# One load instead of two for the query weights, three instead of two for the bias row, in a one-core decode kernel

## Chip, core and metric

The kernel runs on one core of a Trainium2 chip. The time is device microseconds for one execution; lower is better. The core's engines are TensorE (PE), VectorE (DVE), ScalarE (ACT), GpSimd (POOL) and SyncE (SP, which here only issues loads). Data comes from HBM through 16 DMA engines that the core's queues share.

## What is computed

Two branches on the same eight token rows, mixed by a gate. All tensors are bf16.

```python
g = sigmoid((x * gate_w).sum(-1, keepdims=True))        # x: 8 x 1 x 448
q = (x @ wq)                                            # wq: 448 x 4096, 16 heads of 256
k, v = last 1024 of 4096 positions, 8 kv heads, each for 2 query heads
a = softmax(q @ k^T / 16) @ v, then @ wo                # wo: 4096 x 448
b = gelu(layernorm(x) @ w1 + b1) @ w2 + b2              # 448 -> 1792 -> 448
out = g * a + (1 - g) * b
```

## The kernel before, in words

**What is loaded.** Each of the eight batch rows needs 4 MB of keys and 4 MB of values, 64 MB in all. The weights add wq (3.5 MB), wo (3.5 MB), w1 and w2 (1.5 MB each). Nearly everything is read once from HBM.

**The ring of slots.** All large loads go through `ring`, four slots of 32 KB per partition. A list `plan` holds loaders in order: wq, k0, k1, v0, k2, v1, ... k7, v6, w1, v7 with w2, wo. `pump` (L98) issues loaders as long as no more than four slots are unconsumed; `done` (L104) is called by the code that has read a slot, and pumps the next loader. All these loads are issued by SP, in this order, so an issue that waits for a free slot holds every later one of SP's. `half_loader` (L115), `pair_loader` (L125) and `rows_loader` (L137) are the three shapes; the DMA issues stand on L121, L131 and L142. A key or value load is 256 rows of 16 KB.

**Completion semaphores.** In the trace's records the loads of SP and ACT take eight completion semaphores in turn: x, wq's first part, gate_w, wq's second part, wq's last part, k0's two halves, k1, and then the first again for v0, and so on. A load whose semaphore is still in use by an earlier one can't be issued until that one has landed. In the middle of the kernel this never binds; at the end, six of wo's eight pieces wait for it.

**wq.** Its first 384 rows are put three to a partition, `wq_m`, 128 rows of 24 KB that lie one behind the other in HBM. L155 cuts this in two column ranges: the first third (8 KB a row, 1 MB) and the other two thirds (16 KB a row, 2 MB). The last 64 rows of wq (`wq_t`, 128 rows of 4 KB) are a third load. `rows_loader` issues one DMA for each piece.

**The query.** `moments` (L253) turns x into the matmul's stationary tile `xw`. `query` (L383) then runs 24 matmuls of 128x512 on L389, eight for each third of `wq_m`, then four on L401 for `wq_t`, calls `done`, and spreads the result into `qw` (L411 to L427, on ACT and DVE). `gate` (L261) reads g_b, the gate weights that ACT loaded with L185.

**A batch row.** `transpose_keys` (L351) turns the keys, in part by POOL copies (L346), in the main by PE transposes (L370) that ACT (L376) and DVE (L378) copy out of PSUM. `scores` (L429), `top`, `expo`, `turn`, `scale` and `bring` give the softmax, `values` (L501) the product with v. The steps of row b-1 are put between the key blocks of row b, by `steps` (L598).

**The bias row.** `biases` (L189) runs once among row 1's key blocks: SP issues b2 (L190) and then b1 on L194. b1's 1792 elements go as four pieces of 448 elements (896 bytes) to partitions 0, 32, 64 and 96 of `b1_r`, in two loads of two pieces each. `norm` (L303) reads both in row 2 (L317, L318).

**The end.** After the last values, the wide products with w2 and wo accumulate in PSUM, the last chunks in two column halves (L679); L689 adds them, and SP and ACT store a half each (L691).

Of the kernel before, what the change touches and what calls it, by code (L numbers as in the profile page):

```python
# [17 lines left out]
def kernel(  # L18
# [20 lines left out]
    HD = A_wq.shape[1]  # L39
# [6 lines left out]
    QD = 4  # L46
    BL = P // QD
    NJ = Dh // P
    NR = 3
# [97 lines left out]
    wq_m = A_wq[0:DM, :].rearrange("(p r) n -> p (r n)", r=NR)  # L147
# [4 lines left out]
    wo_v = A_wo.rearrange("(q p j) n -> p q (j n)", p=P, j=J8)  # L152
    OW1T = NR * F
    OW2 = OW1T + FH
    wq_r = [wq_m[:, 0:HD], wq_m[:, HD : NR * HD]]  # L155

    def last_values(t):
        pair_loader(A_v_cache, NB - 1, 2)(t)
# [25 lines left out]
    b1_r = consts.tile([P, FQ], BF16)  # L184
# [4 lines left out]
    def biases():  # L189
        nc.sync.dma_start(  # L190
            b2_b[:], B_b2.rearrange("(o d) -> o d", o=1).to_broadcast([NB, D])
        )
        for t in range(0, QD, 2):
            nc.sync.dma_start(  # L194
                b1_r[BL * t : BL * (t + 2) : BL, :],
                B_b1.rearrange("(t d) -> t d", t=QD)[t : t + 2, :],
            )

    ident = consts.tile([P, P], BF16)
# [522 lines left out]
```

## Time and profile before

| what | value |
|---|---|
| time, median of 3 runs | 189.98 us (189.89 to 190.21) |
| time of the profiled execution | 189.76 us |
| its span, first to last instruction | 188.0 us |
| PE busy / DVE / ACT / POOL | 65% / 51% / 49% / 35% of the span |
| loads and stores | 77.85 MB, mean 414 GB/s over the span |
| share of the SP and ACT load queues: SP's queue (q1), ACT's (q10) | 97.3%, 0.0% of 16 engines' span |
| mean granted TensorE clock | 0.873 |

The profiled execution took 1.76 us more than its span; that part lies outside the first and last instruction. Busy times of different engines overlap, so they don't add up to the span. The share of a DMA queue is the time of its packets over the time of all 16 DMA engines.

### The profile page before, as it was taken

To read this page: it belongs to the slowest core of one execution; us is meant where nothing else is said; L and a number is where in the kernel's file an instruction comes from. 1 tells how busy PE (TensorE), PEld (TensorE's weight loads), DVE (VectorE), ACT (ScalarE), POOL (GpSimd) and SP (SyncE) were. 2 spreads that over 40 slices of the span, in tenths; PEclk is the share of its full clock that TensorE was granted. 3 is DMA by queue.
4 is the path that set the end of the run, shared out by engine and by line. 5 is a ranking of instruction groups with operands and counts; after the bars stand their busy time and mean duration, and the time that the engine had idled before them with its cause. 6 is when DMAs were issued, how large, how long until landed. Compare 5 with 4: busy or idle time off the path is not lost.

```text
span 188.0 us, 2799 instructions
## 1 busy us (share of the span) xinstructions
PE 122.3 (65%) x1104; PEld 79.8 (42%) x1104; DVE 96.5 (51%) x166; ACT 91.4 (49%) x115; POOL 66.4 (35%) x143
## 2 busy tenths in 40 slices
PE   0273099598598447991695948923968885353972
PEld 0022096395296216750684336503853662110221
DVE  7306514754287926740673248713763773763511
ACT  2006879598249255862287059620891994010000
POOL 8000093291069505800398039100991840000000
PEclk9999759969969997999579699995799999955599
DMA  6999999999999999999999999999999999999991
GB/s 211 448 411 439 446 422 422 436 443 422 422 439 424 420 436 439 422 422 439 436 425 425 443 432 418 429 443 436 411 436 446 415 425 428 416 429 441 412 402 54
DMA packets 6771, 77.85 MB, mean 414 GB/s; under 512 B 588, under 2 KB 1128, under 8 KB 1896
## 3 DMA queue, kind: packets, MB, share of 16 engines
q1 hardware_dynamic: 6712, 77.68, 97.3%
q8 instruction: 8, 0.13, 0.2%
q10 hardware_dynamic: 48, 0.02, 0.0%
q14 instruction: 3, 0.02, 0.0%
HBM read 77.69 MB, written 0.01 MB: 413 GB/s over the span
## 4 chain that ended last, share of the span: by engine, by line
DMA 76%; PE 13%; POOL 5%; DVE 2%; ACT 1%; issue 1%; SPq 0%; POOLq 0%; DVEq 0%
DMA slot<-in_A_k_cache_dram 51%; DMA slot<-in_A_v_cache_dram 12%; DMA slot<-in_A_wo_dram 9%; PE ktp L370 8%; POOL kt L346 5%; DMA slot<-in_A_wq_dram 5%; DVE kt L378 1%; PE S_ps L435 1%; ACT kt L376 1%; PE S_ps L389 1%; PE S_ps L401 1%; PE PO L506 1%; DVE B L338 1%; PE S_ps L679 0%; SPq L142 0%
## 5 line engine op out<-in xcount | busy, mean ns | idle before, releaser
L370 PE MATMUL ktp<-ident_f,slot 128*128 128x128 f32 x468 | 73.3, 314 | 33.3 <-DMA slot<-in_A_k_cache_dram 21.2
L346 POOL COPY kt<-B 32x128 f32<-32x128 f32 (+1 forms) x128 | 62.1, 485 | 85.9 <-DVE B L338 80.9
L376 ACT COPY kt<-ktp 128x1024 bf16<-128x1024 bf16 x77 | 73.3, 1030 | 27.4 <-PE ktp L370 27.0
L370 PEld LDWEIGHTS ktp<-ident_f,slot 128*128 128x128 f32 x468 | 61.4, 162 | 47.9 <-issue 21.6
L378 DVE COPY kt<-ktp 128x1024 bf16<-128x1024 bf16 x40 | 27.5, 687 | 19.0 <-PE ktp L370 18.9
L435 PE MATMUL S_ps<-kt,qw 128*4 128x512 bf16 x256 | 17.4, 412 | 7.6 <-POOL kt L346 6.2
L506 PE MATMUL PO<-slot,ET 128*16 128x512 bf16 x256 | 17.5, 416 | 7.3 <-DMA slot<-in_A_v_cache_dram 7.3
L453 ACT ACTIVATE E<-S_ps,nmx 128x1024 f32<-128x1024 f32 x8 | 8.9, 1114 | 22.9 <-DVE nmx L448 22.9
L448 DVE TENSOR_REDUCE nmx<-S_ps 128x1 f32<-128x1024 f32 x8 | 9.8, 1224 | 17.9 <-PE S_ps L435 17.9
L338 DVE STREAM_TRANSPOSE B<-slot 128x512 f32<-128x512 f32 (+1 forms) x8 | 7.3, 908 | 21.2 <-DMA slot<-in_A_k_cache_dram 21.2
L506 PEld LDWEIGHTS <-ET 128*16 128x16 bf16 x256 | 7.1, 94 | 16.8 <-issue 11.0
L435 PEld LDWEIGHTS <-qw 128*4 128x4 bf16 x256 | 5.9, 85 | 16.0 <-issue 10.6
L462 DVE STREAM_TRANSPOSE EB<-E 128x1056 f32<-128x1056 f32 x8 | 10.2, 1278 | 0.3
L389 PE MATMUL S_ps<-slot,xw 128*8 128x512 bf16 x24 | 2.9, 617 | 9.4 <-DVE xw L239 6.0
L522 DVE STREAM_TRANSPOSE T<-PO 128x512 f32<-128x512 f32 x8 | 5.6, 703 | 3.6 <-PE PO L506 3.6
L489 DVE TENSOR_TENSOR ET<-sm,mask 128x512 bf16<-128x512 f32 x8 | 5.5, 692 | 3.4 <-PE sm L481 3.4
L414 DVE STREAM_TRANSPOSE qt<-qs 128x512 bf16<-128x512 bf16 x2 | 1.3, 690 | 8.7 <-ACT qs L411 8.7
L389 PEld LDWEIGHTS <-xw 128*8 128x8 bf16 x24 | 0.6, 100 | 10.7 <-POOL b_r L222 5.9
L584 ACT ACTIVATE zb<-za 128x448 f32<-128x448 f32 x1 | 0.6, 577 | 8.5 <-DVE za L583 8.5
L651 PE MATMUL warm<-slot,ident 128*128 128x512 bf16 (+1 forms) x12 | 4.6, 475 | 0.0
L411 ACT ACTIVATE qs<-S_ps 128x1024 bf16<-128x1024 f32 x1 | 1.0, 1023 | 7.3 <-PE S_ps L401 7.3
L468 DVE SCALAR_TENSOR_TENSOR EZ<-EB,gall 128x128 bf16<-128x128 f32 x8 | 4.0, 495 | 0.0
(81 smaller groups left out, 57.6 us busy)
## 6 DMA issues: line engine op xcount, KB each, us to landing
slot<-in_A_v_cache_dram SPq DMA_DIRECT2D x7, 4096.0 KB, 31.1
slot<-in_A_k_cache_dram SPq DMA_DIRECT2D x6, 4096.0 KB, 37.7
slot<-in_A_k_cache_dram SPq DMA_DIRECT2D x4, 2048.0 KB
slot<-in_A_v_cache_dram SPq DMA_DIRECT2D x2, 2048.0 KB
slot<-in_A_wq_dram SPq DMA_DIRECT2D x1, 2048.0 KB
slot<-in_A_wo_dram SPq DMA_DIRECT2D x2, 896.0 KB
slot<-in_B_w_dram SPq DMA_DIRECT2D x1, 1568.0 KB
slot<-in_B_w_dram SPq DMA_DIRECT2D x1, 1344.0 KB, 22.2
```

Source lines behind the costliest of these rows:

```text
L338: nc.vector.transpose(B[:].rearrange("p c w s a -> p (c w s a)"), kn[:, 0 : n * P],)
L346: nc.gpsimd.tensor_copy(words[BL * w : BL * (w + 1), :, 0:n, g * S8 : (g + 1) * S8, 0], B[BL * g : BL * (g + 1), :, w].rearrange("p c s a ...
L370: nc.tensor.transpose(words[:, c, :, 0], kn[:, o : o + P], ident_f[:])
L376: nc.scalar.copy(dst, src)
L378: nc.vector.tensor_copy(dst, src)
L435: nc.tensor.matmul(S_ps[BL * t : BL * t + UR, n * QN : (n + 1) * QN], lhsT=qw[:, j, b, t, rep * u : rep * u + UR], rhs=KT[u][:, t, n * CQ ...
L448: nc.vector.reduce_max(nmx[:], S_ps[:], axis=AXIS.X, negate=True)
L453: nc.scalar.activation(E[:, 0:W], S_ps[:], ACT.Exp, bias=soft.pop(b)[:], scale=1.0, accum_out=total[:],)
L462: nc.vector.transpose(EB[:].rearrange("p c r -> p (c r)"), E[:])
L489: nc.vector.tensor_tensor(ET[:].rearrange("p c u a r -> p (c u) a r"), sm[:] .rearrange("p k (o r) -> p k o r", o=1) .to_broadcast([P, NCK ...
L506: nc.tensor.matmul(PO[BL * t : BL * t + Hq], lhsT=ET[:, c].rearrange("p u a r -> p (u a r)"), rhs=vn[:, c], start=(c < QD), stop=(c >= NCK ...
L522: nc.vector.transpose(T[:, 0 : NG * n], PO[:].rearrange("p u (e j) -> p u j e", j=J8))
```

## The change

wq's two column ranges become one piece, so `rows_loader` issues one DMA of 128 rows of 24 KB, and then `wq_t`. b1's pieces 0 and 1 stay one load; pieces 2 and 3 become one load each.

```diff
-    wq_r = [wq_m[:, 0:HD], wq_m[:, HD : NR * HD]]
+    wq_r = [wq_m]
...
-        for t in range(0, QD, 2):
+        for t, n in ((0, 2), (2, 1), (3, 1)):
             nc.sync.dma_start(
-                b1_r[BL * t : BL * (t + 2) : BL, :],
-                B_b1.rearrange("(t d) -> t d", t=QD)[t : t + 2, :],
+                b1_r[BL * t : BL * (t + n - 1) + 1 : BL, :],
+                B_b1.rearrange("(t d) -> t d", t=QD)[t : t + n, :],
             )
```

The same bytes go to the same places; SP issues one load fewer before k0 and one more behind b2, so from k3 on each load's number in SP's order is what it was.

## The prediction

> **What bounds the kernel.** First the page: the slices, the queues, the chain by engine.
>
> ```profile
> DMA  6999999999999999999999999999999999999991
> ...
> q1 hardware_dynamic: 6712, 77.68, 97.3%
> ...
> DMA 76%; PE 13%; POOL 5%; DVE 2%; ACT 1%; issue 1%; SPq 0%; POOLq 0%; DVEq 0%
> ```
>
> The DMA engines are full in every slice but the first and the last. Then the table of windows (columns: window, length, busy of PE, PEld, DVE, ACT, POOL, clock, DMA share, GB/s):
>
> ```profile
> 0.00:5.00 5.00, 0.00 (x0) 0.00 (x0) 3.89 (x7) 1.28 (x1) 4.29 (x15) 1.00 0.66 228
> 5.00:45.00 40.00, 25.05 (x175) 17.88 (x176) 17.51 (x44) 24.99 (x37) 12.71 (x32) 0.87 1.01 431
> 45.00:90.00 45.00, 30.77 (x318) 20.91 (x317) 24.14 (x36) 24.18 (x31) 16.47 (x32) 0.92 1.01 429
> 90.00:135.00 45.00, 32.12 (x274) 23.74 (x275) 24.51 (x37) 22.91 (x26) 20.12 (x38) 0.81 1.01 430
> 135.00:180.00 45.00, 30.78 (x299) 15.77 (x297) 25.00 (x41) 18.05 (x22) 12.78 (x27) 0.85 1.01 427
> ```
>
> From 5 to 180 us the share is 1.01 and the rate 427 to 431 GB/s: a stream without holes. The packet records say the same: SP's queue holds 182.98 us of packet time per engine, its first packet starts at 1.77 us, and the last load lands at 184.93, so there is room for 183.16 us. What the stream leaves open is its start (the first packets), its end (8 engines land their last load at 184.69 to 184.93, five at 183.33 to 183.56, three between), and the duration of a packet. Last, the timeline of SP, and the chain:
>
> ```profile
> 0.73 1.35 SPq L142 DMA_DIRECT2D slot<-in_A_wq_dram  x3
> ...
> 14.21 0.60 SPq L131 DMA_DIRECT2D slot<-in_A_k_cache_dram  x1
> 32.15 0.60 SPq L131 DMA_DIRECT2D slot<-in_A_v_cache_dram  x1
> 32.79 0.55 SPq L190 DMA_DIRECT2D b_b<-in_B_b_dram  x1
> 33.38 1.14 SPq L194 DMA_DIRECT2D b_r<-in_B_b_dram  x2
> 45.96 0.65 SPq L131 DMA_DIRECT2D slot<-in_A_k_cache_dram  x1
> ```
> ```profile
> 14.21 37.71 DMA slot<-in_A_k_cache_dram
> 51.92 0.14 issue
> ```
>
> The chain calls 37.71 us "DMA k", but k2, issued at 14.21, mostly stands in line: v0, ahead of it, lands at 40.4 to 42.2. So SP refills some 26 us before the engines need it. The next leads are smaller: v1, issued at 32.15, starts when k2 is through at about 50, 18 us; k3 (45.96, v1 lands from 59.94 on) 14 us.
>
> **The change, part by part.**
>
> *wq's packets.* A packet is one row. The records give 309 ns for 8 KB and 611 ns for 16 KB, so 7 ns + 36.9 ns per KB (8 KB more cost 302 ns); 10.5 KB by this is 394 to the measured 404, 7 KB 265 to 272. A 24 KB packet isn't in the trace: by the line it takes 913 ns. Each engine has 8 rows: before 8 x (309 + 611) = 7.36 us and two 9 ns completion writes, after 8 x 913 = 7.30 us and one. With the gaps of 6 ns around a completion write this is 0.07 us less. From both sides: at the 16 KB rate without any fixed part the packet is 906 ns (0.06 us better still), at the 4 KB row's rate (159 ns) 954 ns, 0.26 us worse than before. I take 913, by the nearest row.
>
> *The start.* The first packet of each engine takes 545 to 1085 ns, on average 0.51 us over 309; the second of six engines is up to 0.29 us long, 0.06 us as a mean of all. Together 0.57 us. I take this as a delay of the first bytes, equal for any row length: no change. Otherwise: below.
>
> *SP's issues.* Each takes 0.41 to 0.47 us at the head; one fewer brings `wq_t`, k0, k1, v0 forward by 0.47 us. They stand in line behind 7 us of wq anyway: nothing.
>
> *The query's wait.* Before, eight matmuls run on the first third, from 5.96 to 6.98, and 16 wait:
>
> ```profile
> 5.96 1.02 PE L389 MATMUL S_ps<-slot,xw 128*8 128x512 bf16 x8 [5.96 <-DVE xw L239]
> ...
> 10.44 1.88 PE L389 MATMUL S_ps<-slot,xw 128*8 128x512 bf16 x16 [3.46 <-DMA slot<-in_A_wq_dram]
> ...
> 12.25 1.92 PE L401 MATMUL S_ps<-slot,xw 128*72 128x512 bf16 x4
> ```
>
> After, all 24 wait for the one load. It lands when the second part did (10.40), 0.07 us earlier. 16 matmuls take 1.88 us, so eight more 0.94 us. `wq_t` has landed (11.64) before they are through. The query ends 0.9 us later, with it k2's issue (14.21 to 15.1), the spreading of q, scores(0) and v1's issue (32.15 to 33.1). Behind the waiting matmuls on PE stand k0's transposes (16.55), which are held from 18 to 23 by ACT's queue. All of this costs nothing while the stream covers it: leads of 26, 18 and 14 us against 0.9. It is also gone soon: PE waits 2.49 us for k2's landing ahead of 52.05. If the cover were gone, the price would be 0.9 us at most.
>
> *gate_w.* ACT issues it at 1.36, yet its packets run at 5.42 to 5.72: after the last packet of wq's first part and one packet of the second. The Trainium skill (DMA: Bandwidth & Descriptors, Queues, rings and completion order) says that an engine takes turns between queues only after a group of typically 9 to 17 descriptors; the 8 rows and one completion write here are such a group, and by that rule the longer load holds the other queue for longer. In numbers of the trace: g_b would land at about 11 us (before 6.38 to 6.77), and it is read at 18.51. Nothing.
>
> *The bias row.* One issue more, some 0.55 us, on SP at 34, where SP then idles until 45.96. On the engines: before, each load puts a row on two engines (its semaphore shows two landings); after, engines 0 and 1 get a row of the first, and each one-row load goes to one engine. A row is 41 ns and 9 ns for completion, so one engine can have 0.06 us more than before. The Trainium skill (DMA: Bandwidth & Descriptors, Why a DMA increments its semaphore by 16 and not by 1) puts a load of one row on the lowest-numbered engine; by that rule engine 0 gets both, and there the 0.07 us is used up. The trace agrees as far as it goes: each two-row load had two landings. They land at 60.3 to 60.8 and are read at 64.95: hidden. An extra 0.06 us counts at the end only if that engine is among the eight late ones.
>
> *Semaphores.* Eight in turn: one load less ahead, one more behind b2, so from k3 on each load has the semaphore that it had; wo's pieces, which do wait (at 158.85 to 176.19), are as before. Between, v0 to b1 take a neighbour's: v1 follows wq (landed 10.4), b1's three `wq_t` and k0's halves (by 21.4), later k4 k2 (51.92, issued at 61.79), v3 v1 (61.7, issued at 69.44). All have landed. Nothing.
>
> **Sum.** -0.07 us on the stream, 0 elsewhere: the profiled 189.76 becomes 189.69. The median of the runs is 0.22 us over that execution, so 189.9.
>
> **Rivals.**
>
> 1. *The slow start goes by packet, not by byte* (slower). If the first packet takes 2.66 times its length, as 821 ns against 309 do, a 24 KB one takes 2.43 us, 1.52 over; less the 0.57 and the 0.07 that is +0.88: 190.9. It passes 0.2% from a first packet of about 1.93 us on. Against: later long packets of 8 and 16 KB are all longer by about 0.48 us, whatever their size. 9%.
> 2. *Another engine gets a late packet twice* (slower). The eight late engines are 1.4 us behind: eight 16 KB instruction packets (q8, 880 to 962 ns) each lengthened another engine's stream, three of 8 KB by half of that. If the shifted PE work put two on one engine, the end comes 1.4 us later: 191.3. Against: the same instructions, fetched in the same order. 5%.
> 3. *A load has a price of its own in the stream* (faster). wq's first part could be through at 4.8 and its semaphore came at 5.11 to 5.49. If 0.5 us of that were paid per load, one load less at the head gives 189.4. Against: the next load's packets start at 4.80, 15 ns after the last. By the fixed 2.0 us per transfer of the Trainium skill (DMA: Bandwidth & Descriptors, Anatomy of one DMA, there for transfers issued by GpSimd) this would be 188.0; the trace shows that time beside the next load. 8%.
> 4. *It doesn't do what it says*: the 24 KB row is cut into pieces again. Then the packets stay as they were: 190.0. 7%.
> 5. *x loses its place*: its packets start at 1.69 to 1.76, just ahead of wq's at 1.77. Behind wq's one load it would land near 10, and `xw` (5.96, 3.8 us after x) near 14: the query 4 us later. k2's lead of 26 us and v1's of 18 cover it: 189.9. 5%.
>
> **How the numbers follow.** My case 66%, 4 and 5 add 12%: within 0.2%, 78%; faster 8%; slower 14%. 0.2% (0.38 us) is about what a measurement of this kernel can tell from no change. Predicted 189.9. The range takes in case 3 (189.4), and above it the bad bound of the packet (+0.3) and the runs' spread (+0.23), 190.5; that leaves out 1 and 2, 14%.
>
> **What would show it.** Right: one wq load of 128 packets of about 913 ns after the first, a landing at 10.3, the 24 matmuls in one run from there, k2 issued near 15.1, the DMA share 1.01 from 5 to 180, k2 landing at 51.9, last load at 184.9. Wrong: first packets over 1.9 us, packets of 8 or 16 KB for `wq_m`, an engine 2 us behind, a slice under 9 in the middle, or SP waiting for a semaphore at a place where it hadn't.

## The result, and the profile after

The changed kernel takes 190.22 us (189.98 to 190.41, 22 runs), the kernel before 189.95 us (189.78 to 190.21, 22 runs): 1.0013 times as long, 95% interval 1.0007 to 1.0019. That is within 0.2%, but not within the noise, and it is slower where the forecast was 0.07 us faster. The profiled execution took 190.19 us, its span is 188.5 us.

The windows of the changed kernel, with the same columns:

```profile
0.00:5.00 5.00, 0.00 (x0) 0.00 (x0) 3.88 (x7) 1.28 (x1) 4.29 (x15) 1.00 0.71 223
5.00:45.00 40.00, 24.58 (x162) 18.08 (x162) 16.81 (x43) 22.84 (x35) 12.77 (x32) 0.87 1.00 429
45.00:90.00 45.00, 32.42 (x330) 21.37 (x330) 23.80 (x37) 26.09 (x33) 16.56 (x33) 0.91 1.01 430
90.00:135.00 45.00, 31.85 (x268) 25.27 (x269) 24.53 (x36) 22.38 (x26) 19.66 (x37) 0.80 1.01 431
135.00:180.00 45.00, 31.52 (x304) 17.06 (x302) 24.97 (x42) 18.69 (x22) 13.38 (x28) 0.83 1.00 426
```

From 5 us on the stream is as full as before, 426 to 431 GB/s at a share of 1.00 to 1.01. So no new hole opened; what differs must lie in the first 5 us or behind 180. The share of the first window has even gone up, 0.66 to 0.71. Its rate, 228 before and 223 here, can't be compared: the view counts a packet whole in the window in which it starts, and a second trace of the changed kernel shows 232. Long packets need the packet records, below.

The timeline at the head and at the end of the changed kernel:

```profile
0.73 0.86 SPq L142 DMA_DIRECT2D slot<-in_A_wq_dram  x2
...
11.24 2.73 PE L389 MATMUL S_ps<-slot,xw 128*8 128x512 bf16 x24 [11.24 <-DMA slot<-in_A_wq_dram]
...
13.90 1.92 PE L401 MATMUL S_ps<-slot,xw 128*72 128x512 bf16 x4
...
15.85 0.60 SPq L131 DMA_DIRECT2D slot<-in_A_k_cache_dram  x1
...
186.10 0.32 SPq L691 DMA_DIRECT2D out_dram<-res  x1
```

and the store of the kernel before:

```profile
185.68 0.32 SPq L691 DMA_DIRECT2D out_dram<-res  x1
```

The 24 matmuls are in one run, as forecast, but from 11.24 and not from 10.3. The last engine brought its part of the same 3 MB 0.8 us later than before (11.20 against 10.40); the mean of the 16 engines is 0.2 us later. The store is 0.42 us later. These are single executions, and the one profiled before, 189.76, lies 0.19 us below its kernel's median; the medians differ by 0.27 us.

The packet records say where this comes from. In the changed kernel the first packet of each engine took 1422 to 2486 ns, on average 1786, where 912 ns is what a 24 KB packet takes later on. Counting each packet's bytes evenly over its time, wq's stream had moved 1.041 MB by 5 us before and 0.948 MB after, and 2.316 against 2.234 MB by 8 us: 0.08 MB, which at 429 GB/s is 0.19 us. k1's parts land on the 16 engines at 30.73 to 31.08 before, mean 30.93, and at 30.73 to 31.89 after, mean 31.14. The last load of all lands at a mean of 184.25 before and 184.43 after, its last engine at 184.93 and 185.35. So in these two traces 0.2 us are lost ahead of k1's landing, and a full stream doesn't give them back.

### The profile page after: what moved, and what is told of

It is laid out like the page before. It is cut to its first block, busy times and chain, and to the rows that moved or that the text cites. A ratio compares the mean times of both kernels' runs of the same rounds, so it can differ in the third digit from the quotient of the medians.

```text
span 188.5 us, 2800 instructions
## 1 busy us (share of the span) xinstructions
PE 124.2 (66%) x1104; PEld 83.3 (44%) x1104; DVE 95.4 (51%) x166; ACT 91.3 (48%) x115; POOL 66.7 (35%) x143
## 4 chain that ended last, share of the span: by engine, by line
DMA 76%; PE 11%; POOL 5%; DVE 3%; ACT 2%; issue 1%; POOLq 0%; DVEq 0%
DMA slot<-in_A_k_cache_dram 50%; DMA slot<-in_A_v_cache_dram 12%; DMA slot<-in_A_wo_dram 9%; DMA slot<-in_A_wq_dram 6%; PE ktp L370 6%; POOL kt L346 5%; ACT kt L376 2%; PE S_ps L389 1%; DVE kt L378 1%; PE S_ps L435 1%; PE S_ps L401 1%; PE PO L506 1%; DVE EB L462 1%; DVE B L338 1%; PE S_ps L679 0%
## 5 line engine op out<-in xcount | busy, mean ns | idle before, releaser
L370 PE MATMUL ktp<-ident_f,slot 128*128 128x128 f32 x468 | 75.4, 322 | 31.1 <-DMA slot<-in_A_k_cache_dram 18.5
L370 PEld LDWEIGHTS ktp<-ident_f,slot 128*128 128x128 f32 x468 | 64.3, 167 | 44.7 <-issue 19.0
L414 DVE STREAM_TRANSPOSE qt<-qs 128x512 bf16<-128x512 bf16 x2 | 1.3, 690 | 10.3 <-ACT qs L411 10.3
L411 ACT ACTIVATE qs<-S_ps 128x1024 bf16<-128x1024 f32 x1 | 1.0, 1024 | 8.9 <-PE S_ps L401 8.9
## 6 DMA issues: line engine op xcount, KB each, us to landing
slot<-in_A_wq_dram SPq DMA_DIRECT2D x1, 3072.0 KB, 10.5
```

Source lines behind the costliest of these rows:

```text
L370: nc.tensor.transpose(words[:, c, :, 0], kn[:, o : o + P], ident_f[:])
```

## The experiments

The theories: **first packet** (long rows as the very first work of the engines move less in the first microseconds), **bias row** (the one-row loads put more on one engine), **late query** (the query's delay reaches the end). One measure serves for all runs: the mean over the 16 engines of k1's landing. In the two kernels it lies behind wq, ahead of the issue of the bias row (b1 at 33.38 and 35.30), and ahead of the first packet of the queue that fetches instructions (q8, at 34.87 and 36.60). So it shows the loss at the start alone. Each landing is that of one profiled execution. Traces with the same loads ahead of k1 agree within 0.07 us (30.93 and 31.00 with those of before, 31.14, 31.11 and 31.12 with those of the changed kernel), so smaller differences say nothing. Each ratio is against the kernel before on the same chip; the variants have 5 to 11 runs each.

| run | first load | k1's mean landing, us | median, us | ratio, 95% interval |
|---|---|---|---|---|
| before | 8 KB rows of wq | 30.93 | 189.95 | 1 |
| changed | 24 KB rows of wq | 31.14 | 190.22 | 1.0013 (1.0007 to 1.0019) |
| after_again | the same | 31.11 | 190.24 | 1.0013 (1.0004 to 1.0022) |
| e1_first16 | 16 KB of each wq row | 31.07 | 190.11 | 1.0008 (0.9999 to 1.0017) |
| e2_first4 | 4 KB of each wq row | 31.26 | 190.24 | 1.0017 (1.0008 to 1.0027) |
| e3_tail_first | wq's last part, 4 KB rows | 30.81 | 189.70 | 0.9989 (0.9980 to 0.9997) |
| e3_again | the same | 30.82 | 189.69 | 0.9987 (0.9978 to 0.9996) |
| e4_query_late | as before | 31.00 | 189.91 | 0.9997 (0.9989 to 1.0006) |
| e5_bias_pairs | 24 KB rows of wq | 31.12 | 190.54 | 1.0031 (1.0018 to 1.0043) |
| e6_first_half_k | 512 bytes of each wq row | 31.46 | 190.66 | 1.0037 (1.0025 to 1.0050) |
| e7_tail_first_two | wq's last part, 4 KB rows | 30.85 | 189.81 | 0.9992 (0.9983 to 1.0001) |
| e8_bias_two | 24 KB rows of wq | 31.24 | 190.32 | 1.0020 (1.0011 to 1.0028) |
| e9_key_first | 16 KB rows of k0 | 31.36 | 190.25 | 1.0014 (1.0005 to 1.0023) |
| e10_close_rows | 16 rows of 24 KB | 37.11 | 196.05 | 1.0315 (1.0301 to 1.0329) |

But for e5 and e9, and e4's 0.07 us, the two columns move together: a start that lands k1 0.1 us later makes the kernel 0.1 to 0.2 us longer.

A second measure takes the late beginning of an engine and its long first packet together: the moment at which the first packet ends, less the time that a packet of this length takes later, averaged over the first 16 packets of SP's queue. With 24 KB rows first it is 2.75 to 2.80 us in four traces (changed, after_again, e5, e8), with 16 KB 2.65 in both (e1, e9), with 8 KB 2.48 and 2.50 (before, e4). With 4 KB it is 2.36 where the rows lie 24 KB apart (e2), and 1.97 to 2.14 where they lie one behind the other (e3, e3_again, e7). So 24 KB rows at the beginning cost 0.25 to 0.32 us more than 8 KB rows, whichever of these traces are compared. What the packets behind them lose (e2, e6, e9) isn't in it.

**e1_first16**, the cut in the other place:

```diff
-    wq_r = [wq_m[:, 0:HD], wq_m[:, HD : NR * HD]]
+    wq_r = [wq_m[:, 0 : 2 * HD], wq_m[:, 2 * HD : NR * HD]]
```

> wq in two loads as before, but cut the other way: 16 KB rows first, then 8 KB; the bias row as before. Three theories of the 0.27 us. First packet: an engine's first packet is slow by its length, and what is lost there is never made up. The first packets lost 0.57 us per engine with 8 KB rows (with the second packets) and 0.90 us with 24 KB; 16 KB should lie between, about 0.73, so about 0.15 us over before, 190.1, ratio 1.0008, with first packets of 1.2 to 1.4 us. Bias row: the extra one-row loads are the cause, so no difference, 1.0000. Late query: 16 matmuls can start at about 8 and only eight wait for the rest, so the query ends about 0.9 us earlier than before: no difference or faster, 1.0000 or less.

The ratio is the one that the first-packet theory gave, 1.0008, but the interval just holds 1. The packets were not as expected, so this agreement is partly luck: on average 1017 ns, 608 to 1802, but engines began on average at 2.25 us instead of 1.96. The loss is partly a later beginning, so the duration of packets alone is no measure of it.

**e2_first4**, 4 KB and then 20 KB:

```diff
-    wq_r = [wq_m[:, 0:HD], wq_m[:, HD : NR * HD]]
+    wq_r = [wq_m[:, 0 : HD // 2], wq_m[:, HD // 2 : NR * HD]]
```

> wq in two loads, 4 KB rows first, then 20 KB; the bias row as before. First packet: shorter first packets lose less, 0.3 to 0.5 us per engine where 8 KB lost 0.57, so 0.1 to 0.2 us under before, 189.8, unless the second packets (20 KB) are now the ones that the start makes long, then like before or worse. Bias row: no difference. Late query: all 24 matmuls wait for the second load's landing at about 10.4, the query ends 0.9 us later than before, of 1.6 in the changed kernel: about 0.15 us slower, 1.0008.

Slower than before by 1.0017, not faster: a miss for the plain form of the theory, with the exception that it had named. The first packets took 542 ns on average instead of 159, and the 20 KB packets that began from 3 to 4 and from 4 to 5 us took 811 and 828 instead of 761.

**e3_tail_first**, the changed kernel with `wq_t` ahead:

```diff
-    add(("wq",), rows_loader(wq_r + [wq_t]))
+    def wq_loader(t):
+        nc.sync.dma_start(t[:, NR * HD : NR * HD + HD // 2], wq_t)
+        rows_loader(wq_r)(t)
+    add(("wq",), wq_loader)
```

> The changed kernel, with wq's last part (4 KB rows, 0.5 MB) issued ahead of the single load of 24 KB rows instead of behind it; the bias row in three loads, as in the changed kernel. First packet: the 24 KB packets are no longer the first, so the loss at the start goes back to 0.3 to 0.6 us per engine: 189.7 to 190.0, ratio to before 0.999 to 1.000. Bias row: as slow as the changed kernel, 190.2, 1.0013. Late query: the query now waits for the single load's landing at about 11.3 in place of 11.2 and ends where it did in the changed kernel: 190.2, 1.0013.

This separates the theories best: the 24 KB load, the three bias loads and a late query are all there, and the kernel is 0.21 us faster than before. Chain, matmuls, k2's issue and store:

```profile
1.19 10.39 DMA slot<-in_A_wq_dram
...
11.62 2.73 PE S_ps L393 x18
14.35 1.87 PE S_ps L405 x4
16.23 35.65 DMA slot<-in_A_k_cache_dram
```
```profile
185.60 0.32 SPq L695 DMA_DIRECT2D out_dram<-res  x1
```

The 24 KB load lands by 11.58 with 0.5 MB more ahead of it; those take 1.22 us at 429 GB/s, so without them it would be 10.4, where the old second part was. The query is later than in the changed kernel (k2 issued at 16.23 against 15.85), and the store comes at 185.60, before that of either kernel. The first packets took 318 ns on average instead of 159, the first three 24 KB packets of an engine 1031, 980 and 941 instead of 912: the start still costs, but less. By 5 us the stream had moved 1.106 MB. Repeated on another chip (e3_again), the kernel comes out the same: 0.9987, k1 at 30.82.

**e4_query_late**, the kernel before with another order of wq's thirds:

```diff
-        for r in range(NR):
+        for r in (1, 2, 0):
...
-                        start=(r == 0),
+                        start=(r == 1),
```

> The kernel before, its loads untouched; only the query takes wq's thirds in the order 2, 3, 1, so that all 24 matmuls wait for the second load, as they wait in the changed kernel for the only one. First packet and bias row: no difference, 1.0000, while the query ends some 0.9 us later. Late query: 0.9 of the changed kernel's 1.6 us, so about 0.15 us slower, 1.0008.

No difference, but a weaker test than planned: the 24 matmuls ran from 10.64 to 13.37, yet the last four took 1.07 us in place of 1.92, and k2's issue came only 0.2 us later, at 14.40. e3 (k2 at 16.23) and e9 (at 19.40) are the evidence against the late query.

**e5_bias_pairs**, the single wq load with two bias loads, and b2 in two:

```diff
-    wq_r = [wq_m[:, 0:HD], wq_m[:, HD : NR * HD]]
+    wq_r = [wq_m]
...
-        nc.sync.dma_start(
-            b2_b[:], B_b2.rearrange("(o d) -> o d", o=1).to_broadcast([NB, D])
-        )
+        for h in (0, NB // 2):
+            nc.sync.dma_start(
+                b2_b[h : h + NB // 2, :],
+                B_b2.rearrange("(o d) -> o d", o=1).to_broadcast([NB // 2, D]),
+            )
```

> The changed kernel's single load of 24 KB rows, but the bias row in two loads as before; so that the number of loads stays, b2 is issued in two loads of four partitions each. First packet: as slow as the changed kernel, 1.0013 over before, 190.2. Bias row: back to before, 1.0000 (or 0.07 us under).

Slower than either theory said. Up to the store it equals after_again: k1's mean 31.12 to 31.11, the last load's mean 184.42 to 184.41, and the store is issued at 186.03 in both. The profiled spans, 188.6 and 188.4, part in the closing barrier, where VectorE arrives at 188.28 instead of 187.89. Why is open; in these two traces the loads land alike. The time of e5 therefore decides nothing on the bias row, and e8 tests it again.

**e6_first_half_k**, 512 bytes of each row first:

```diff
-    wq_r = [wq_m[:, 0:HD], wq_m[:, HD : NR * HD]]
+    wq_r = [wq_m[:, 0 : HD // 16], wq_m[:, HD // 16 : NR * HD]]
```

> wq's 384 rows in two loads, 512 bytes of each 24 KB row first and then the other 23.5 KB; the bias row as before. It parts two readings of the loss at the start. By length: an engine's first packets lose by their bytes, so 512-byte packets lose little, and the second load, issued 0.4 us behind, is the first with long packets: its first packets lose what the changed kernel's did unless the start is over by then; 190.0 to 190.2, with 23.5 KB packets of over 1.2 us. By place: the first touch of rows that lie 24 KB apart over 3 MB costs, whatever is read of them; then the 512-byte packets take several times their normal 20 to 25 ns and the long ones that follow run at once at about 890 ns; 190.0 to 190.3. The packets tell which, the time less so.

The 512-byte packets took 25 to 61 ns, all of them, so touching the first 512 bytes of each row is not the cost. The first 23.5 KB packet of each engine, from 2.2 us on, took 1038 to 2259 ns, on average 1673, where 893 is normal: nearly as slow as the changed kernel's first, though the rows had been touched. The time, 190.66, is beyond what either reading gave; by 5 us only 0.797 MB had moved.

**e7_tail_first_two**, e3's order with the old 8 KB and 16 KB loads and two bias loads (the edit is e3's, on the kernel before).

> The kernel before with wq's last part (4 KB rows that lie one behind the other, 0.5 MB) issued first, then the 8 KB and 16 KB columns; the bias row as before. If what made the tail-first kernel 0.2 us faster than before is its gentle start, this one is as fast, 0.9990, 189.7, or 0.07 us behind it for its 128 packets more. If it was the single load, no difference to before.

0.9992, k1 at 30.85: as expected if the order alone brings most of e3's gain, though the interval (0.9983 to 1.0001) just holds 1. By the medians e3 is 0.11 us ahead of it, for which the working had 0.07 us (128 packets and a load less); the two intervals overlap widely, so this difference is not shown.

**after_again**, the changed kernel unchanged.

> The changed kernel again, on the chip of the three beside it: 1.0013 over before, first packets of 1.4 to 2.5 us, and k1's last part landing 0.5 us or more behind that of before (31.07).

1.0013 again. First packets of 0.91 to 2.09 us, on average 1516 ns against 1786, but begun later, at 2.15 on average against 1.90; k1's last engine lands at 31.84. The loss is there in both profiled executions of the changed kernel; late beginnings and long packets share it differently.

**e8_bias_two**, the single wq load, the bias row as before, `wq_t` in two:

```diff
-    wq_r = [wq_m[:, 0:HD], wq_m[:, HD : NR * HD]]
+    wq_r = [wq_m]
...
-    add(("wq",), rows_loader(wq_r + [wq_t]))
+    add(("wq",), rows_loader(wq_r + [wq_t[:, 0 : HD // 4], wq_t[:, HD // 4 : HD // 2]]))
```

> The changed kernel's single load of 24 KB rows at the very beginning, the bias row in two loads exactly as before; so that the number of loads stays, wq's last part, which follows, is cut in two loads of 2 KB rows (128 packets more, 0.06 us). First packet: as slow as the changed kernel, 190.2 to 190.3, 1.0013 to 1.0017 over before. Bias row: back to before, 1.0000.

1.0020 (1.0011 to 1.0028), k1 at 31.24. Without the bias part of the change the kernel is as slow as with it, also when the 0.06 us are taken off that the cut of `wq_t` was reckoned to cost: the bias row is not the cause. The changed kernel says the same: k1 has landed late there before b1 is issued at 35.30.

**e9_key_first**, the first half of k0 ahead of wq:

```diff
-    add(("wq",), rows_loader(wq_r + [wq_t]))
-    add(("k", 0), half_loader(A_k_cache, 0))
+    kept = []
+    def k_around_wq(t):
+        for i in range(NG):
+            v = A_k_cache[0, i:Hkv:NG, kv_base:Sk, :].rearrange(
+                "a (s c) d -> s a (c d)", c=NCK
+            )
+            nc.sync.dma_start(t[:, i * HS : (i + 1) * HS], v)
+            if i == 0:
+                rows_loader(wq_r + [wq_t])(kept[0])
+    add(("wq",), kept.append)
+    add(("k", 0), k_around_wq)
```

> The kernel before, with the first half of k0 (16 KB rows, which lie one behind the other in stretches of 512 KB) issued ahead of wq's three loads instead of behind them; the bias row as before. The query comes some 5 us later, which the earlier runs say costs nothing while k2's issue stays ahead of 40. First packet by length: like the kernel that began with 16 KB of each wq row, 190.1, 1.0008. By place (rows 24 KB apart of which a part is read are the cost, rows one behind the other are not): like the two that began with wq's last part, 189.8, 0.9992. Late query: 5 us late, so well over 1.002.

Slow, with rows that lie one behind the other, but not a clean case for length. SP's first issue took 0.62 us (0.41 for wq), and the engines began at 2.27 on average, 0.31 us behind before. Yet those of e1 began at 2.25 and k1 landed at 31.07 there, so a late beginning doesn't explain 31.36. The first packets end as e1's do (2.65 by the second measure); the next 16 packets are slower, 729 ns on average against e1's 646 (normal 611). Why is open. The query's end is 5 us later, and the time is no longer than the landing says: the leads cover even that.

**e10_close_rows**, 16 rows and then 112:

```diff
-    add(("wq",), rows_loader(wq_r + [wq_t]))
+    def wq_loader(t):
+        nc.sync.dma_start(t[0:16, 0 : NR * HD], wq_m[0:16, :])
+        nc.sync.dma_start(t[16:P, 0 : NR * HD], wq_m[16:P, :])
+        nc.sync.dma_start(t[:, NR * HD : NR * HD + HD // 2], wq_t)
+    add(("wq",), wq_loader)
```

> wq's 384 rows as 24 KB rows, but in two loads: the first 16 of the 128 rows (one for each engine, 384 KB that lie close together), then the other 112; wq's last part and the bias row as before. By length: the first packets are 24 KB, as in the changed kernel, and take 1.4 to 2.5 us, so 190.2, 1.0013. By place: the first packets lie within 384 KB, as close as those of wq's last part (4 KB rows), and so start as gently, with packets of about 1.1 us: 189.7 to 189.9, 0.999.

It told nothing on its question. The windows of this run:

```profile
0.00:5.00 5.00, 0.00 (x0) 0.00 (x0) 2.80 (x7) 1.28 (x1) 4.29 (x15) 1.00 0.90 154
5.00:10.00 5.00, 0.00 (x0) 0.00 (x0) 1.87 (x7) 0.29 (x1) 0.00 (x0) 1.00 0.87 237
10.00:15.00 5.00, 0.00 (x0) 0.00 (x0) 0.00 (x0) 0.00 (x0) 0.00 (x0) 1.00 0.95 241
...
20.00:180.00 160.00, 107.33 (x1006) 76.38 (x1006) 86.16 (x144) 89.50 (x113) 62.24 (x128) 0.88 1.01 430
```

The engines are busy (0.87 to 0.95) and move half: all 24 KB packets of both loads took 1.1 to 2.9 us, long after the start. With the partitions split 16 and 112 both loads were slow themselves, and the 6 us are the price.

## Why the prediction was wrong, point by point

- **What bounds the kernel: right.** The stream is full from 5 to 180 us in every run but e10, and a start that lands k1 later lengthens the kernel by about that.
- **wq's packets: right.** 912 ns against 913 worked out. The straight line through 8 and 16 KB holds from 512 bytes to 24 KB, but its price is 37.75 ns for a KB of 1024 bytes; the working's 36.9 ns is for 1000 bytes, and with it 10.5 and 7 KB seemed to miss (394 for 404, 265 for 272). Rightly counted the line gives 403 and 271. That the 0.07 us come back as time is not shown: e3 and e7 differ by 0.11 us, within their intervals.
- **The start: the step that failed.** "I take this as a delay of the first bytes, equal for any row length: no change." It is not equal. With the 24 KB rows first, the first microseconds move 0.08 MB less and k1 lands 0.21 us later. With the 0.07 us that the packets give, the term is about 0.28 us where I had 0; the ends of the first packets say 0.25 to 0.32. Issued behind 0.5 MB of 4 KB rows, the same load doesn't make the kernel slower than before (e3), and the bias part taken out leaves the loss (e8). The reading of the kernel before had also missed that some engines began late, at 2.27 us and behind, one of them with a first packet of 520 ns, under the 545 given; the mean of 0.51 us over 309 ns stands. The rival "by packet, not by byte" had the place and the sign, at 9%, and a price three times too high: 2.43 us for the first packet, which took 1.79 on average, and +0.88 us where +0.27 came. Its condition, a first packet over 1.93 us, was met on 5 of 16 engines. That 190.22 lies inside the range, 189.4 to 190.5, is luck as far as this term goes: the room above was made for a slower packet rate and the spread of the runs.
- **The query: right on the price, wrong on the size.** Its end came 1.64 us later, 0.8 of it from the later landing. It cost nothing, and 5 us cost nothing either (e9).
- **The bias row and the semaphores: right.** The three issues took 1.33 us, SP idled behind them until 47.97, and wo's pieces wait where they did. e8 shows that the bias row isn't the cause.
- **gate_w: right that it is hidden, wrong on how.** Its packets began at 5.40 to 6.69, in the middle of wq's load, not behind it. By the rule of the Trainium skill (DMA: Bandwidth & Descriptors, Queues, rings and completion order) an engine would have finished wq's 8 rows first; here engines turned to it after some four of them, at about the time at which they did before.
- **The chances.** 78% on "within 0.2%" rested on a stream that is full; the one place where it isn't, I had measured, and then carried over without a row for it. Two first-packet rows (8 KB, and the small ones of x) can't say how a longer row behaves.

What makes long rows slow while the engines begin is open. It isn't the touch of each row's first bytes (e6), and not the length of the very first packet alone (e2 and e7 both begin with 4 KB rows and land k1 0.41 us apart). What fits the runs but e10 is that long packets which many engines begin together within the first 1 to 1.5 us of the stream are slow, the longer the more (8, 16 and 24 KB). How far apart the rows lie, and how late the first packets come, play a part that these runs don't separate.

## What to carry to other kernels

Where a stream of loads bounds the kernel and is full from then on, an edit of the first loads acts through the first microseconds. Measure these by a landing that lies behind all edited loads, averaged over the engines, and not by packet durations alone. Here a merge that was to save 0.07 us of packets cost about four times that at the very beginning; one load later the same merge cost nothing. Of the loads that are needed first, try the one that is small and lies in one piece ahead of the others: here wq's last part first and then one load of 24 KB rows is 0.25 us faster than the kernel before (0.9987, 0.9978 to 0.9996) and, by the medians, 0.5 us faster than the changed one.

## What the runs showed of the hardware that was not expected

- Loads of 16 and of 112 partitions with the same 24 KB rows ran at 154 to 241 GB/s, their packets at 1.1 to 2.9 us, where the load of 128 partitions took 912 ns a packet. The Trainium skill (DMA: Bandwidth & Descriptors, The descriptor swizzle) describes for 128 partitions that each engine writes through a port of its own; that the other splits lose this is a guess that no run here shows.
- A skew between engines lasts. k1's 16 engines landed 0.34 us apart before and 1.16 us apart after; each instruction packet of 16 KB (eight in a run, 0.88 to 0.97 us) holds one more engine back by about 1.4 us to the end. Before, the first comes at 34.87, and of the next load to land, v0, 15 engines are through by 40.81 and one at 42.23. So the last load's landings spread over 1.6 us before, and over 2.1 us after.
- One kernel (e5) lost 0.2 us in the closing barrier, in the one trace that was taken: store at 186.03 as in after_again, spans 188.6 and 188.4.
